# Loading q and k of six retention steps in natural order of heads, with a PSUM bank of its own for the state's products

## The chip, the cores and the metric

The kernel runs on one core of a Trainium2 chip. The metric is the device time of one execution in microseconds (us). Before the change three runs took 658.92, 657.10 and 658.42 us, median 658.42 us. One more execution was recorded by the hardware profiler.

The engines are named as in the profile: PE (TensorE; PEld is its weight load), DVE (VectorE), ACT (ScalarE), POOL (GpSimd) and SP (SyncE, which here only issues transfers).

## The reference

```
# retention, batch 4, heads 8, sequence 768, head size 64
state = zeros(B, H, D, D)
for t in range(S):
    state = gamma[h] * state + k[:, :, t] (outer) v[:, :, t]
    y[:, :, t] = q[:, :, t] @ state / sqrt(D)
# then a feed-forward block on x = y as (3072, 512)
h = x @ w_in                  # 512 x 2048
g = h / (1 + exp(-1.702 * h))
out = g @ w_out               # 2048 x 512
```

gamma is 1 - 2^-(5+h) of head h. The data are float32; the two weight matrices reach the kernel as 64-bit values, which it narrows to float32 on the chip.

## The kernel before

**Tiles.** The sequence is cut into 12 chunks of 64 positions; one step works on one chunk of two batches, all eight heads. There are 24 steps. Steps 0 to 11 are batches 0 and 1, steps 12 to 23 are batches 2 and 3. Four steps make a block of 512 tokens, and the feed-forward block follows on such blocks (up, gate, down), with products saved by Strassen-like sums.

**Two layouts.** Steps 0 to 5 (`j < NEW`, NEW = 6) hold q, k and v with the position on the partitions: partitions 0 to 63 are the first batch, 64 to 127 the second; the eight heads lie along the free dimension. From step 6 on, the partition halves are groups of four heads instead, and q and k are loaded already turned. `halves_anew` (L938) moves the state, the mask and the decays from the one layout to the other, once, after step 5.

**One step of the first layout**, in the names of the code:
- `load` (L131): q on SP's queue, k on POOL's queue (step 0: ACT's), v on SP's queue (L146). For q and k each batch half goes in two transfers, one per group of four heads, and they interleave the groups, so that head n of the tile is head s of group 0, then head s of group 1. v goes in natural order, one transfer a half.
- `turn` (L246): PE transposes pairs of neighbouring heads of the tile (L255); `turned` copies them from PSUM on ACT (L266). With the interleaved order a pair is heads s and s + 4.
- `decay` (L268): ACT scales k by the chunk's decay, one instruction a head (L277).
- `attend` (L286) puts the products on PE, 16 of 64x64x64 each: attention scores (L294), the state's update k'v (L302), the share of y that comes from the old state (L311) and the local share (L317). The array is used as four tiles, rows half by columns half. Scores and update go to the two banks of `pa`, both shares of y to the two banks of `py`. In all four groups the row half decides the bank, and every group uses all four tiles.
- `masked` (L321), `by_state` (L326), `output` (L338) and `updated` (L366) run on DVE, `aged` (L356) on ACT (steps 0 to 5).

**PSUM.** `pa` and `py` hold two banks each. The remaining four are `ps`: two tags, `x` and `y`, of two buffers in turn. Transposes use `y`; the feed-forward's up products `ph` use `x` and `y` (`unit`, L981).

**What sets the order.** PE's and most other instructions around the change are kept in program order (`pin`). For steps 0 to 7 that order is written out by hand, as a list of names (L997 to L1015): for example `step5-4` is the scores of step 5 with the rest of step 4, `step-3` the rest of step 3 alone, `turn`, `turned`, `decay`, `masked`, `state`, `x`, `aged`, `updated` are the functions above, `up0.th.p` and `gate0.th.p` are an up product and its gate, `w3a` a load of weights (L186), and `abs3`, `half3`, `rest3` the parts of its narrowing (ACT L212, DVE L216 to L227). The narrowed weights' raw bytes go through three buffers (`RAWS`, L175), so that a weight load waits for an earlier narrowing. The change leaves this list alone.

Of the kernel before, what the change touches and what calls it, by code (L numbers as in the profile page):

```python
# [9 lines left out]
F32 = mybir.dt.float32  # L10
U32 = mybir.dt.uint32
AF = mybir.ActivationFunctionType
ALU = mybir.AluOpType
P = 128
# [14 lines left out]
def kernel(  # L29
# [94 lines left out]
    def pin(i):  # L124
        return tc.keep_in_program_order(i) if ordered[0] else i


    NEW = 6
    QKV = {}

    def load(j, what="qkv"):  # L131

        b, c = j // NC * 2, j % NC
        rows = slice(c * D, (c + 1) * D)
        keep = tc.keep_in_program_order if j < 2 * CB else lambda i: i

        def plain(name, src, tag, bufs, engine=sp):
            t = two.tile([P, H, D], F32, name=name + "_in", tag=tag, bufs=bufs)  # L140
            QKV[name, j] = t
            for i in range(2):
                if j < NEW:
                    to, at = t[i * D:(i + 1) * D], src[b + i, :, rows, :].rearrange("h p d -> p h d")
                    for n in range(1 if name == "v" else 2):
                        keep(engine.dma_start(*((to, at) if name == "v" else (to[:, n:H:2], at[:, n * HP:(n + 1) * HP]))))  # L146
                else:
                    for r in range(2):
                        keep(engine.dma_start(t[r * D:(r + 1) * D, i * HP:(i + 1) * HP],
                                              src[b + i, r * HP:(r + 1) * HP, rows, :].rearrange("h p d -> p h d")))  # L150

        if j < NEW:
            if "q" in what:
                plain("q", q, "q_sq", 2)
            if "k" in what:
                plain("kn", k, "k_sq" if j in (0, 1, 4, 5) else "o", 2, pool if j else act)
        elif "q" in what:
            for name, src in (("q", q), ("k", k)):
# [70 lines left out]

    QT, KT, KD, AT, TURNED, PA, PU, PY, SHARE = [{} for _ in range(9)]
    HALF = [slice(i * D, (i + 1) * D) for i in range(2)]
    TWO = [(i, r) for i in range(2) for r in range(2)]

# [32 lines left out]
    def decay(j):  # L268

        if j % NC == NC - 1:  # L270
            return
        KD[j] = home(j, "kd")
        x = QKV["kn", j]
        if j < NEW:

            for h in range(H):
                pin(act.activation(KD[j][:, h], x[:, h % HP * 2 + h // HP], AF.Copy, scale=cold[:, H + h:H + h + 1]))  # L277
        else:
            pin(pool.tensor_mul(KD[j].rearrange("p (i s) d -> p i s d", i=2), x.rearrange("p (i s) d -> p i s d", i=2),
                                cold[:, None, H:H + HP, None].to_broadcast([P, 2, HP, D])))  # L280

    def by_half(t, j):

        return t.rearrange("p s (w t) -> p w s t" if j < NEW else "p (w s) t -> p w s t", w=2)

    def attend(j, f=None):  # L286

        pa = ps_a.tile([P, 2, 2, HP, D], F32, name="pa", tag="pa")
        if j is not None:
            PA[j] = pa  # L290
            kt, qt = by_half(KT.pop(j), j), by_half(QT[j], j)
            for s in range(HP):
                for u, w in TWO:
                    pe.matmul(pa[HALF[w], u, 0, s, :], kt[HALF[u], w, s, :], qt[HALF[u], w, s, :], start=True, stop=True)  # L294
        if f is not None:
            c = f % NC
            old, vn, a, qt = state[c % 2], QKV.pop(("v", f)), AT.pop(f), by_half(QT.pop(f), f)
            if c < NC - 1:
                kd = KD.pop(f)
                for s in range(HP):  # L300
                    for w, u in TWO:
                        pe.matmul(pa[HALF[u], w, 1, s, :], kd[HALF[w], HP * u + s, :], vn[HALF[w], HP * u + s, :],  # L302
                                  start=True, stop=True)


            py = ps_a.tile([P, 2, 2, 4, D], F32, name="py", tag="py")
            if c:
                for s2 in range(2):
                    for w in range(2):
                        for u, o in TWO:  # L310
                            pe.matmul(py[HALF[o], u, 1, 2 * w + s2, :], old[HALF[u], w, 2 * s2 + o, :],  # L311
                                      qt[HALF[u], w, 2 * s2 + o, :], start=True, stop=True)
            for s2 in range(2):
                for u in range(2):
                    for w, o in TWO:
                        s = 2 * s2 + o
                        pe.matmul(py[HALF[o], w, 0, 2 * u + s2 if f < NEW else 2 * s2 + u, :],  # L317
                                  vn[HALF[w], HP * u + s, :], a[HALF[w], u, s, :], start=True, stop=True)
            PU[f], PY[f] = pa[:, :, 1], py

    def masked(j):  # L321
        AT[j] = home(j, "at")
        pin(dve.tensor_mul(AT[j], PA.pop(j)[:, :, 0],
                           mask if j < NEW else mask[:, 0:1].to_broadcast([P, 2, HP, D])))

    def by_state(f):  # L326

        if f < NEW:
            SHARE[f] = tmp = two.tile([P, 2, 4, D], F32, name="tmp", bufs=1)
            pin(dve.tensor_mul(tmp.rearrange("p i a t -> p i (a t)").rearrange("p i (r t) -> p i r t", r=2),  # L330
                               PY[f][:, :, 1].rearrange("p r (i s) t -> p i r (s t)", i=2),
                               rowd.rearrange("p (r s) t -> p r (s t)", r=2)[:, None].to_broadcast([P, 2, 2, P])))
        else:
            SHARE[f] = tmp = two.tile([P, 4, 2, D], F32, name="tmp", bufs=1)
            pin(dve.tensor_mul(tmp.rearrange("p a i t -> p i a t"), PY[f][:, :, 1],
                               rowd[:, None].to_broadcast([P, 2, HP, D])))

    def output(f):  # L338
# [14 lines left out]
        else:  # L353
            pin(act.activation(x, y, AF.Copy))

    def aged(f):  # L356

        c = f % NC
        old, new = state[c % 2], state[(c + 1) % 2]
        if f < NEW:  # L360
            for s in range(HP):
                pin(act.activation(new[:, :, s], old[:, :, s], AF.Copy, scale=whole[:, s:s + 1]))
        else:
            pin(pool.tensor_mul(new.rearrange("p r s d -> p (r s) d"), old.rearrange("p r s d -> p (r s) d"),
                                whole_h[:, :, None].to_broadcast([P, H, D])))

    def updated(f):
        c = f % NC
        new, u = state[(c + 1) % 2], PU.pop(f)
        if c == 0:  # L370
            pin(dve.tensor_copy(new, u))
        elif c < NC - 1:
            pin(dve.tensor_add(new, new, u))
# [553 lines left out]
    def lay_whole():  # L927

        for r in range(2):
            pin(pool.dma_start(  # L930
                whole[HALF[r]], bass.AP(tensor=col_decay.tensor, offset=col_decay.offset + (D - 1) * W + H + HP * r,
                                        ap=[[0, D], [1, HP]])))

    def late_loads():
        load(2 * CB, "qkv")
# [2 lines left out]
    def halves_anew():  # L938

        pin(pool.dma_start(whole_h, bass.AP(tensor=col_decay.tensor, offset=col_decay.offset + (D - 1) * W + H,  # L940
                                            ap=[[0, P], [1, H]])))
        pool.tensor_copy(mask[HALF[1], 0], mask[HALF[1], 1])
        pool.tensor_copy(cold[HALF[1], H:H + HP], cold[HALF[1], H + HP:2 * H])
        old, new = state[NEW % NC % 2], state[(NEW + 1) % NC % 2]
        for u in range(2):
            pool.dma_start(new[HALF[1 - u], u], old[HALF[u], 1 - u])
        for u in range(2):
            pool.tensor_copy(old[HALF[u], 1 - u], new[HALF[u], 1 - u])

    works |= {  # L950

# [159 lines left out]
```

## Time and profile before

| | before |
|---|---|
| median of three runs | 658.42 us |
| the profiled execution's own time | 659.02 us |
| its span | 657.3 us |
| PE busy | 639.0 us (97%) |
| DVE busy | 437.9 us (67%) |
| ACT, POOL busy | 166.6 us, 182.0 us |
| DMA packets | 148149, 131600 of them under 512 B |

The span runs from the program's first instruction to its last; 1.7 us of the execution lie outside it. The page divides the span into 40 slices of 16.4 us and gives each engine's busy share in tenths, the clock that was granted to PE, and the mean busy share of the 16 DMA engines. An engine's idle time costs something only where the end of the program follows from it. PE's busy time is that of pipelined products, so a busy PE may still be slowed by a lower clock. The chain of work that ended last follows from each instruction back to what released it; it names a DMA where a landing was waited for, and a queue (SPq, ACTq) where an issue was.

### The profile page before, as it was taken

What the parts mean: (1) busy time and instruction counts of PE and PEld (TensorE: products, weight loads), DVE (VectorE), ACT (ScalarE), POOL (GpSimd) and SP (SyncE); (2) the same over time, 40 slices, a digit from 0 to 9 for tenths busy, and PEclk for the clock granted to TensorE, in tenths of its full rate; (3) what the DMA queues carried; (4) which work ended last, traced back from release to release, by engine and by line L of the source; (5) the groups of instructions that cost most, each with busy time, mean ns of one, the idle gap of its engine ahead of it and who ended that gap; (6) DMA issues with size and microseconds to landing.
All of it is one profiled execution on the core that took longest, in us unless ns stands there. A gap on an engine that the chain in (4) does not pass through costs nothing.

```text
span 657.3 us, 15175 instructions
## 1 busy us (share of the span) xinstructions
PE 639.0 (97%) x6390; PEld 577.0 (88%) x6390; DVE 437.9 (67%) x609; ACT 166.6 (25%) x320; POOL 182.0 (28%) x210
## 2 busy tenths in 40 slices
PE   6789999999999999999999999999999999999997
PEld 2678888888888888889999888999888999988997
DVE  3699989999936963348885246987245986144854
ACT  4574334551000000333100333110333110333210
POOL 6400311310478218000636200535300334300000
PEclk9899999999999999999999999999999999999999
DMA  9997549854233465541567821387831244501142
GB/s 168 189 256 207 152 102 233 220 127 62 49 92 146 119 155 150 192 135 42 155 161 205 246 40 49 114 196 180 257 59 49 77 140 153 205 24 49 52 158 97
DMA packets 148149, 89.77 MB, mean 137 GB/s; under 512 B 131600, under 2 KB 134416, under 8 KB 147056
## 3 DMA queue, kind: packets, MB, share of 16 engines
q1 hardware_dynamic: 135856, 44.66, 30.3%
q0 software_dynamic: 9456, 38.16, 18.5%
q10 hardware_dynamic: 2768, 5.96, 2.6%
q8 instruction: 50, 0.82, 0.5%
q14 instruction: 19, 0.16, 0.1%
HBM read 71.32 MB, written 14.94 MB: 131 GB/s over the span
## 4 chain that ended last, share of the span: by engine, by line
PE 89%; DMA 6%; DVE 2%; SPq 1%; issue 0%; ACT 0%; ACTq 0%; DVEq 0%
PE pq L717 27%; PE px L590 17%; PE pd L852 15%; PE pz L590 8%; PE ph L488 6%; PE ph L417 4%; PE py L590 4%; DMA W<-in_moe_w_in_dram 2%; PE pa L294 2%; PE py L317 1%; DMA G<-in_moe_w_in_dram 1%; PE py L311 1%; DMA W<-in_moe_w_out_dram 1%; PE pa L302 1%; PE pb L488 1%; DMA kn_in<-in_k_dram 1%
## 5 line engine op out<-in xcount | busy, mean ns | idle before, releaser
L692 POOL DMA_DIRECT2D LATE<-W2D x28 | 15.5, 555 | 245.6 <-PE pq L717 124.0
L717 PE MATMUL pq<-W,G 128*128 128x128 f32 x672 | 80.2, 276 | 0.0
L717 PEld LDWEIGHTS pq<-W,G 128*128 128x128 f32 x672 | 77.6, 192 | 0.6
L590 PE MATMUL px<-X,W1A 128*128 128x256 f32 x256 | 60.5, 379 | 0.0
L590 PE MATMUL px<-X,LATE 128*128 128x256 f32 x256 | 60.5, 379 | 0.0
L717 PE MATMUL pq<-LATE 128*128 128x128 f32 x448 | 59.8, 276 | 0.0
L417 PE MATMUL ph<-X,W1A 128*128 128x256 f32 x256 | 57.4, 382 | 1.2 <-DVE X L352 0.8
L417 PEld LDWEIGHTS ph<-X,W1A 128*128 128x128 f32 x256 | 48.0, 190 | 8.1 <-DVE X L352 0.9
L717 PEld LDWEIGHTS pq<-LATE 128*128 128x128 f32 x448 | 54.5, 192 | 0.4
L590 PEld LDWEIGHTS px<-X,LATE 128*128 128x128 f32 x256 | 48.6, 190 | 6.6
L590 PEld LDWEIGHTS px<-X,W1A 128*128 128x128 f32 x256 | 48.4, 190 | 6.5
L852 PE MATMUL pd<-W,G 128*128 128x256 f32 x224 | 49.6, 381 | 0.0
L852 PEld LDWEIGHTS pd<-W,G 128*128 128x128 f32 x224 | 42.2, 190 | 5.9
L398 ACT ACTIVATE G<-G 128x512 f32<-128x512 f32 x49 | 30.8, 629 | 45.3 <-DVE G L645 19.7
L635 DVE TENSOR_TENSOR G<-pz,vv 128x512 f32<-128x512 f32 x16 | 11.1, 692 | 46.7 <-ACT vv L605 46.6
L852 PE MATMUL pd<-W,LATE 128*128 128x256 f32 x160 | 35.2, 380 | 0.0
L852 PEld LDWEIGHTS pd<-W,LATE 128*128 128x128 f32 x160 | 30.2, 190 | 4.3 <-DVE LATE L574 0.2
L739 ACT ACTIVATE o<-pq 128x512 f32<-128x512 f32 (+1 forms) x14 | 7.6, 545 | 91.3 <-PE pq L717 91.3
L590 PE MATMUL pz<-X,W1A 128*128 128x256 f32 x128 | 30.3, 379 | 0.0
L590 PE MATMUL py<-X,W1A 128*128 128x256 f32 x128 | 30.2, 379 | 0.0
L590 PE MATMUL pz<-X,LATE 128*128 128x256 f32 x128 | 30.2, 379 | 0.0
L717 PE MATMUL pq<-W,LATE 128*128 128x128 f32 x224 | 29.7, 275 | 0.1
(210 smaller groups left out, 1169.6 us busy)
## 6 DMA issues: line engine op xcount, KB each, us to landing
LATE<-W2D POOLq DMA_DIRECT2D x28, 768.0 KB, 4.8
W<-in_moe_w_in_dram SPq DMA_DIRECT2D x12, 512.0 KB, 5.2
W<-in_moe_w_out_dram SPq DMA_DIRECT2D x10, 512.0 KB, 5.7
out_dram<-o POOLq DMA_DIRECT2D x20, 256.0 KB, 3.5
q_sq<-in_q_dram SPq DMA_DIRECT2D x144, 32.0 KB, 2.3
k_sq<-in_k_dram SPq DMA_DIRECT2D x144, 32.0 KB, 2.2
v_in<-in_v_dram SPq DMA_DIRECT2D x72, 64.0 KB, 2.7
LATE<-W1D ACTq DMA_DIRECT2D x3, 1536.0 KB, 7.4
```

The source lines that it names most:

```text
L294: pe.matmul(pa[HALF[w], u, 0, s, :], kt[HALF[u], w, s, :], qt[HALF[u], w, s, :], start=True, stop=True)
L302: pe.matmul(pa[HALF[u], w, 1, s, :], kd[HALF[w], HP * u + s, :], vn[HALF[w], HP * u + s, :], start=True, stop=True)
L311: pe.matmul(py[HALF[o], u, 1, 2 * w + s2, :], old[HALF[u], w, 2 * s2 + o, :], qt[HALF[u], w, 2 * s2 + o, :], start=True, stop=True)
L398: pin(act.activation(g, h[:, i], AF.Gelu_apprx_sigmoid))
L417: pe.matmul(h[:, ab], w, X[:, 2 * th + c // 2, c % 2, :], start=(ab == 0 and c == 0), stop=(c == 3), skip_group_check=True)
L488: pe.matmul(acc[:, u, :], w, x, start=(start and u == 0 and c == 0), stop=(stop and c == 1), skip_group_check=True)
L590: pe.matmul(acc[:, u, :], w1(2 * d + u, sw)[:, c, :], X[:, sx, c, :], start=(start and u == 0 and c == 0), stop=(stop and c == 1), skip_gr ...
L635: dve.tensor_add(a[3], z, v)
L692: engine.dma_start(c, W2D[i])
L717: pe.matmul(p0[:, j, :], a[:, d], w[:, d], start=(new and j == 0 and d == 0), stop=(d == NP // 2 - 1), skip_group_check=True)
L739: act.activation(to, y, AF.Copy)
L852: pe.matmul(p0[:, n, :], g1(m, p, sa)[:, n * P:(n + 1) * P], W2[:, sb, p, :], start=(new and p == 0 and n == 0), stop=(last and p == NP - ...
```

## The change

The loads of q and k of steps 0 to 5 take the heads as they lie: one transfer for each batch half instead of two, 24 transfers less (12 on SP's queue, 10 on POOL's, 2 on ACT's), each of 128 KB instead of 64 KB. A tile then pairs heads 2s and 2s+1. The partition half u of the state holds heads 2s + u instead of 4u + s, and what depends on it follows: the mask is read in another order, `whole` is loaded with a step of two, the update's products take head 2s + u.

With this pairing the old state's share of y must land on the partition half that its head's state lies on, so each of those 16 products goes from row half u to column half u. They get a bank of their own, `sr`, out of the pool `ps` (tag `x` in steps 1 to 3, `y` in steps 4 and 5), and DVE reads it there. The products' order becomes: update, the old state's share, the local share, as before. `held` gives the buffer that holds the state; from step 6 on the two buffers change places, because `halves_anew` now writes all four quarters to the other buffer (two by DMA, in runs of 256 B, two by POOL's copies, which no longer read what the DMAs write).

```
@@ load
-                    for n in range(1 if name == "v" else 2):
-                        keep(engine.dma_start(*((to, at) if name == "v" else (to[:, n:H:2], at[:, n * HP:(n + 1) * HP]))))
+                    keep(engine.dma_start(to, at))
@@ decay
-                pin(act.activation(KD[j][:, h], x[:, h % HP * 2 + h // HP], AF.Copy, scale=cold[:, H + h:H + h + 1]))
+                pin(act.activation(KD[j][:, h], x[:, h], AF.Copy, scale=cold[:, H + h:H + h + 1]))
@@ attend
-            old, vn, a, qt = state[c % 2], QKV.pop(("v", f)), AT.pop(f), by_half(QT.pop(f), f)
+            old, vn, a, qt = held(f), QKV.pop(("v", f)), AT.pop(f), by_half(QT.pop(f), f)
...
-                        pe.matmul(pa[HALF[u], w, 1, s, :], kd[HALF[w], HP * u + s, :], vn[HALF[w], HP * u + s, :],
+                        h = 2 * s + u if f < NEW else HP * u + s
+                        pe.matmul(pa[HALF[u], w, 1, s, :], kd[HALF[w], h, :], vn[HALF[w], h, :],
                                   start=True, stop=True)
             py = ps_a.tile([P, 2, 2, 4, D], F32, name="py", tag="py")
+            PU[f], PY[f] = pa[:, :, 1], py
+            if f < NEW:
+                if c:
+                    SR[f] = sr = ps.tile([P, 2, HP, D], F32, name="sr", tag="x" if f < CB else "y")
+                for s in range(HP if c else 0):
+                    for w in range(2):
+                        for u in range(2):
+                            pe.matmul(sr[HALF[u], w, s, :], old[HALF[u], w, s, :], qt[HALF[u], w, s, :],
+                                      start=True, stop=True)
+                for s in range(HP):
+                    for w, u in TWO:
+                        pe.matmul(py[HALF[u], w, 0, s, :], vn[HALF[w], 2 * s + u, :], a[HALF[w], u, s, :],
+                                  start=True, stop=True)
+                return
@@ masked
-                           mask if j < NEW else mask[:, 0:1].to_broadcast([P, 2, HP, D])))
+                           m3.rearrange("p (s u) t -> p u s t", u=2) if j < NEW else mask[:, 0:1].to_broadcast([P, 2, HP, D])))
@@ by_state
-            pin(dve.tensor_mul(tmp.rearrange("p i a t -> p i (a t)").rearrange("p i (r t) -> p i r t", r=2),
-                               PY[f][:, :, 1].rearrange("p r (i s) t -> p i r (s t)", i=2),
-                               rowd.rearrange("p (r s) t -> p r (s t)", r=2)[:, None].to_broadcast([P, 2, 2, P])))
+            pin(dve.tensor_mul(tmp, SR.pop(f), rowd[:, None].to_broadcast([P, 2, HP, D])))
@@ aged, updated
+    def held(f, n=0):
+
+        return state[(f + n + (f >= NEW)) % 2]
...
@@ lay_whole: offset "+ r" and step 2 in place of "+ HP * r" and step 1
@@ halves_anew
-        old, new = state[NEW % NC % 2], state[(NEW + 1) % NC % 2]
+        old, new = held(NEW - 1, 1), held(NEW).rearrange("p r (s u) d -> p u (r s) d", u=2)
         for u in range(2):
             pool.dma_start(new[HALF[1 - u], u], old[HALF[u], 1 - u])
         for u in range(2):
-            pool.tensor_copy(old[HALF[u], 1 - u], new[HALF[u], 1 - u])
+            pool.tensor_copy(new[HALF[u], u], old[HALF[u], u])
```

More of the change, by code (lines that the diff above doesn't have):

```diff
@@ L227, in rest @@
             pin(dve.tensor_add(self.w, b, a))
-    QT, KT, KD, AT, TURNED, PA, PU, PY, SHARE = [{} for _ in range(9)]
+    QT, KT, KD, AT, TURNED, PA, PU, PY, SR, SHARE = [{} for _ in range(10)]
     HALF = [slice(i * D, (i + 1) * D) for i in range(2)]
@@ L316, in attend @@
                         s = 2 * s2 + o
-                        pe.matmul(py[HALF[o], w, 0, 2 * u + s2 if f < NEW else 2 * s2 + u, :],
+                        pe.matmul(py[HALF[o], w, 0, 2 * s2 + u, :],
                                   vn[HALF[w], HP * u + s, :], a[HALF[w], u, s, :], start=True, stop=True)
-            PU[f], PY[f] = pa[:, :, 1], py
     def masked(j):
@@ L354, in output @@
             pin(act.activation(x, y, AF.Copy))
+    def held(f, n=0):
+        return state[(f + n + (f >= NEW)) % 2]
     def aged(f):
-        c = f % NC
-        old, new = state[c % 2], state[(c + 1) % 2]
+        old, new = held(f), held(f, 1)
         if f < NEW:
@@ L368, in updated @@
         c = f % NC
-        new, u = state[(c + 1) % 2], PU.pop(f)
+        new, u = held(f, 1), PU.pop(f)
         if c == 0:
@@ L930, in lay_whole @@
             pin(pool.dma_start(
-                whole[HALF[r]], bass.AP(tensor=col_decay.tensor, offset=col_decay.offset + (D - 1) * W + H + HP * r,
-                                        ap=[[0, D], [1, HP]])))
+                whole[HALF[r]], bass.AP(tensor=col_decay.tensor, offset=col_decay.offset + (D - 1) * W + H + r,
+                                        ap=[[0, D], [2, HP]])))
     def late_loads():
```

## The prediction

> **What bounds the kernel now.** I read the page's engine shares and slices first, to see where PE is idle; then the stretches that this suggests; then the chain in order of time, for what ends the waits there; then the transfers and the products that are edited.
>
> ```profile
> PE 639.0 (97%) x6390; PEld 577.0 (88%) x6390; DVE 437.9 (67%) x609; ACT 166.6 (25%) x320; POOL 182.0 (28%) x210
> ...
> PE   6789999999999999999999999999999999999997
> ...
> DVE  3699989999936963348885246987245986144854
> ```
>
> PE is busy everywhere but in the first three slices (49 us). The same in stretches (PE, PEld, DVE, ACT, POOL busy us; granted clock; DMA share; GB/s):
>
> ```profile
> 2.00:4.00 2.00, 0.10 (x1) 0.10 (x1) 0.00 (x0) 0.16 (x1) 1.92 (x6) 1.00 0.70 147
> 4.00:10.00 6.00, 3.47 (x8) 1.55 (x9) 0.00 (x0) 1.32 (x2) 4.71 (x8) 1.00 1.07 207
> 10.00:19.00 9.00, 8.98 (x112) 5.05 (x110) 5.32 (x8) 5.57 (x20) 5.46 (x9) 1.00 1.25 183
> 19.00:29.00 10.00, 6.22 (x172) 5.48 (x173) 6.63 (x11) 5.81 (x13) 5.39 (x9) 0.83 1.19 210
> 29.00:37.00 8.00, 5.69 (x134) 4.82 (x137) 7.28 (x9) 6.98 (x24) 0.00 (x0) 1.00 1.07 237
> ```
>
> From 4 to 37 us the transfers keep the 16 DMA engines over 100% busy (packets overlap); from 37 to 60 PE (21.73 of 23 us) and DVE (21.33) are both near full, and so to 94; after that PE alone carries the time. So an edit counts by how much earlier or later PE passes 94 us. The chain (start, us, what) names what paces the front:
>
> ```profile
> 10.12 8.73 DMA W<-in_moe_w_in_dram
> ...
> 18.87 9.45 DMA G<-in_moe_w_in_dram
> ...
> 31.91 5.24 DMA W<-in_moe_w_in_dram
> ```
>
> The reader is to see three landings in a row, w0a, w2a and w3a of the weights (ahead of w0a stands k of step 0, 6.29 us to its landing at 9.46). ACT's L212 and DVE's L216 to L227 narrow each, and from w2a on (half2 starts at 29.58) DVE hardly rests until 92. Their issues wait too: SP and ACT share eight semaphores in turn, so an issue waits for the landing of the transfer eight before it. w2a went out at 18.87 because w0a landed at 18.85.
>
> **The transfers.** Issue costs, ns, min/median/max:
>
> ```profile
> L146 SPq DMA_DIRECT2D q_in<-in_q_dram x24: 596/615/3915, 0.8 to 36.0; - x24
> L146 POOL DMA_DIRECT2D kn_in<-in_k_dram x20: 617/627/717, 3.8 to 25.5; - x20
> L146 SPq DMA_DIRECT2D v_in<-in_v_dram x12: 596/602/1213, 6.9 to 44.2; - x12
> ```
>
> v's 128 KB costs one issue of 0.6 us, like q's 64 KB. The change therefore takes 12 x 0.615 = 7.4 us off SP's queue, 10 x 0.627 = 6.3 us off POOL's and 2 x 0.69 (ACT's median) = 1.4 us off ACT's. But issue is not what these transfers spend their time on: q's take a median 6.2 us from issue to landing, v's 8.2, k's on POOL 7.2, so a queue of work stands before the DMA engines. Bytes and the 256 B runs stay. An issue that leaves a full queue earlier lands no earlier.
>
> The queue isn't full at the start. From 2 to 4 us only 147 GB/s moved, at a share of 0.70, while SP and ACT put out 64 KB per 0.65 us each. With 128 KB an issue, this stretch could move the 207 GB/s of the next: (207 - 147) x 2 us = 0.12 MB, or 0.6 us at 190 GB/s. w0b goes out at 2.3 instead of 3.80, behind two issues instead of four. And SP no longer stands between w0a and w2b: a dip near 20 us, where w2b has just been issued (17.74, landing 24.81), may fill for some 0.3 us. I take 0.9 us earlier for w0a, w2a and w3a alike. The ends: nothing (0), if DMA's work after 4 us is all that counts; and 3.9 us, if w0a lands as much earlier as it is issued (four issues of 0.6 us and a 1.9 us wait of SP's for k of step 0 go; it would leave near 6.2 instead of 10.12).
>
> POOL's queue: `causal`, which ends at 15.33, comes about 1 us earlier with w0b, then `whole` (2 x 0.55), k3 (2 x 0.63) and k of steps 4 and 5, which go out at 16.6 to 18.5 instead of 18.8 to 26. These 512 KB now compete with w2b and w2a. Of them 384 KB landed after w2a's 28.31; at 210 GB/s they are 1.8 us. I take nothing, since POOL's transfers are in flight throughout 18 to 33 us in either order and share with SP's by turns; at worst w2a is 1.8 us later, 0.9 net of the gain.
>
> ACT loses two issues before L952, hidden: ACT then waits for w0b until 10.19. k of step 0 lands near 6 instead of 9.46, and the turn of step 0, `rows` and the scores of step 0 move up by some 3 us; but step 1's scores (21.93) wait for DVE's `updated0` (21.10), queued behind half0a, which waits for w0a. So PE only waits longer there. Its granted clock is already at half from 21.6 to 25.0, after 2.95 us of idling (L294 takes 1.06 instead of 0.62 us for PE's advance); a longer idle time may stretch that by one such period, which the wait for w2a's narrowing covers (PE idles 0.81 us at 28, DVE 1.56 us at 29.6): 0, at worst 0.6.
>
> The trace puts the price on the engines, 256 B at a time. The Trainium skill, "DMA: Bandwidth & Descriptors", Rules for kernel authors, says to coalesce many small transfers, as below 64 KB one pays mostly for overhead. By that rule alone SP's 7.4 us would be the gain.
>
> **The products of the old state.** Here the change adds work. Step 5's, from the order of time (start, busy us):
>
> ```profile
> 70.37 0.65 PE L311 MATMUL py<-G,state 64*64 64x64 f32 x32
> ...
> 70.83 0.65 PE L317 MATMUL py<-G,v_in 64*64 64x64 f32 x32
> ...
> 71.55 0.69 DVE L330 TENSOR_TENSOR tmp<-py,rowd 128x512 f32<-128x512 f32 x1 [0.68 <-PE py L317]
> ```
>
> 16 products are 32 instructions and advance PE by 0.47 us (70.37 to 70.83), on four array tiles: eight each, 59 ns apart. `sr` uses two tiles, so 16 each: 0.94 us, 0.47 more, in steps 1 to 5. The ends: 0, if the 14.7 ns from one instruction to the next is an issue limit; and 32 x 59 = 1.89 us, 1.42 more, if the two row halves also can't write one bank together, which no group of this trace does. I take 0.47, the nearest reading.
>
> Where it lies: in step 1 PE then waits for X until 28.08 (0.81 us idle), in step 2 for `updated2` until 36.73 (1.17), in step 3 for rest3 until 44.89 (0.36 after 0.17): covered, exactly in step 3. Step 4's 0.47 at 54.5 is on PE's unbroken path to step 5. There DVE waits 0.68 us for L317, since `py` was one tile; now it needs `sr` alone, which ends at 70.31 + 0.47 + 0.94 = 71.72, plus 0.03 for the start: 71.75 against 71.55, +0.2. Behind that wait stand `updated5`, `output`, rest4, the weight issue at 76.58 and the q and k loads that SP issues after it; k lands at 92.0 and L258 lets PE go on at 94.11 after 0.89 idle. PE itself arrives 0.94 later, at 94.16. So +0.2 at 94 us. If DVE did not wait there, the cover of 0.89 would be gone all the same and the sum would be +0.05.
>
> The Trainium skill, "TensorEngine Tiling (Array Packing)", Gotcha 1, speaks against this: row tiles write different PSUM banks and can't access one bank at the same time. By it the 1.89 us would hold; by the row, 0.94. Here the two row tiles write different partitions of the bank, of which the page says nothing.
>
> **Banks.** `sr` takes turns in `x` and `y`. Its tightest waits: `up0.0.2` (37.36) then needs `gate0.0.0` done (35.02), `up0.1.2` (about 48.5) `state3` (45.44), step 5's `sr` (70.3) `state4` (60.93). Cost 0 with 2.3 us to spare; if PE's part came 2.3 us earlier than ACT's, the difference.
>
> **The rest.** L277, L323 and L330 keep counts and shapes (0.34 us a head, 0.69 and 0.69 us); L352, already strided, takes the same 0.68, so other strides cost 0 (0 to 0.1 each). In `halves_anew` POOL's copies lose a wait of 1.72 us for the DMAs, whose runs get shorter (2.15 us to landing, at worst 1 more); their reader, step 7's part at 94, is 15 us off. 0.
>
> Sum: -0.9 + 0.2 = -0.7 us, or 659.02 - 0.7 = 658.3 for the profiled execution (span 657.3 and 1.7 around it). That one is 0.6 above the median, so 657.7 against 658.42.
>
> **The rivals.** A: the issues were the limit, not the engines. For it: w2a's issue waits on w0a's landing. Against it: DMA shares of 1.07 to 1.25, landings 6 to 9 us after issue. w0a 3.9 us earlier, +0.2: 654.7.
> B: row halves serialise on `sr`'s bank, and the kernel gets slower. Step 3 loses 1.1 of its 1.42 us (0.53 covered, 0.25 left from step 2), and in step 5 `sr` ends at 70.78 + 1.42 (step 4's) + 1.42 = 73.62, where DVE starts now at 71.55: +2.1. Together +3.2 - 0.9: 660.7. It decides from 0.73 us more a group, some 1.2 us for the 32 instructions, where the total passes zero.
> C: POOL's earlier k loads delay w2a by 1.8, and with it DVE's unbroken work: +0.9 + 0.2: 659.5.
> D: the transfers are hidden entirely, only +0.2 stays: 658.6.
>
> **How the numbers follow.** Forecast 0.33, A in whole or in part 0.23, B 0.19, C 0.13, D 0.12. About 0.3% (2.0 us) is what a measurement of this kernel tells from no change. Faster by more: most of A, some of the forecast, 0.26. Slower by more: most of B, a third of C, 0.25. Same: 0.49. The range runs from most of A, 655.0, to B, 661.0; the forecast's own is 656.5 to 659.
>
> **What would show it.** Right: w0a and w2a issued 4 us earlier or more, but landing within 1.5 us of before; `sr`'s 32 instructions in 0.9 us; DVE's wait for PE at step 5 below 1 us; PE past 94 at 93 to 94. Wrong: a landing of w2a outside 26.8 to 29.8, a group of 1.4 us or more, or a new idle time of PE before an `up0` product that waits for a bank.

## The result, and the profile after

| | before | after |
|---|---|---|
| median | 657.76 us (6 runs, 654.84 to 658.92) | 662.91 us (6 runs, 661.23 to 664.35) |
| ratio | | 1.0082, interval 1.0056 to 1.0107 |
| the profiled execution | 659.02 us, span 657.3 | 662.38 us, span 660.7 |
| DMA packets | 148149 | 147765 |

The kernel is slower by 5 us, where 0.7 us less was forecast and 661.0 was the upper end of the range. The two medians for before (here six runs, the prediction had three) differ by 0.66 us; single runs of one kernel lie up to 3.9 us from their median (before: 2.9), and a trace shows one run.

The page's shares and slices after the change, the same rows as before:

```profile
PE 643.0 (97%) x6390; PEld 581.2 (88%) x6390; DVE 437.2 (66%) x609; ACT 166.6 (25%) x320; POOL 177.2 (27%) x200
...
PE   6799999999999999999999999999999999999997
...
DVE  3589889999936874357885246986245986144854
```

PE has the same number of instructions and is busy 4.0 us longer. The rows below name two things that fit, a lower clock and the state's products on two tiles; their shares were not measured. The stretches of the front (PE, PEld, DVE, ACT, POOL busy us; granted clock; DMA share; GB/s):

```profile
2.00:4.00 2.00, 0.10 (x1) 0.11 (x1) 0.00 (x0) 1.48 (x2) 1.92 (x6) 1.00 0.85 164
4.00:10.00 6.00, 3.73 (x10) 1.81 (x10) 0.39 (x1) 1.10 (x3) 2.52 (x4) 1.00 1.14 212
10.00:19.00 9.00, 8.27 (x110) 4.51 (x109) 6.23 (x11) 6.54 (x23) 5.72 (x9) 1.00 1.15 173
19.00:29.00 10.00, 5.85 (x145) 5.34 (x149) 4.63 (x8) 3.05 (x8) 2.03 (x3) 0.73 0.88 183
29.00:37.00 8.00, 8.00 (x95) 6.69 (x89) 6.99 (x9) 7.49 (x24) 0.00 (x0) 0.69 1.06 202
```

Up to 10 us the transfers run as foreseen: 164 and 212 GB/s, against 147 and 207. Then 173 against 183, and from 19 to 29 us the DMA share is 0.88 where it was 1.19, with 183 GB/s instead of 210. PE's clock was at half from 20.2 to 23.6 and from 27.1 to 33.9; before only from 21.6 to 25.0.

The chain in order of time (start, us, what):

```profile
1.60 7.59 DMA kn_in<-in_k_dram
...
16.41 12.85 DMA G<-in_moe_w_in_dram
...
32.95 7.20 DMA W<-in_moe_w_in_dram
```

The second is w2a, as before. It leaves 2.46 us earlier (16.41, was 18.87) and takes 12.85 us instead of 9.45, so that it lands 0.95 us later. w3a (the third) lands at 40.16, 3.0 us later. From there the delay is carried to the end almost unchanged: the scores of step 7 start at 96.84 instead of 94.11, the first `pq` product at 310.36 instead of 307.63 (2.73 both), the span ends 3.36 later.

**The hole.** Between w2a's issue and its landing something takes the DMA engines away. The stretches in single microseconds, after:

```profile
18.00:19.00 1.00, 0.27 (x20) 0.13 (x10) 0.93 (x3) 0.99 (x4) 1.00 (x3) 1.00 0.79 11
19.00:20.00 1.00, 0.00 (x0) 0.01 (x1) 0.88 (x2) 0.81 (x2) 1.00 (x2) 1.00 0.00 0
20.00:21.00 1.00, 0.98 (x33) 0.88 (x33) 0.00 (x0) 0.00 (x0) 0.34 (x1) 0.62 0.99 1
21.00:22.00 1.00, 1.00 (x7) 1.00 (x6) 0.93 (x2) 0.00 (x0) 0.47 (x1) 0.50 0.46 56
```

and the same of before:

```profile
18.00:19.00 1.00, 0.98 (x60) 0.84 (x52) 0.00 (x0) 0.13 (x1) 1.00 (x3) 1.00 1.30 183
19.00:20.00 1.00, 0.00 (x0) 0.00 (x0) 0.43 (x1) 1.00 (x3) 1.00 (x2) 1.00 1.32 181
20.00:21.00 1.00, 0.00 (x0) 0.00 (x0) 0.94 (x2) 0.99 (x4) 0.14 (x1) 1.00 0.95 187
21.00:22.00 1.00, 0.07 (x4) 0.10 (x7) 0.78 (x2) 0.74 (x2) 0.08 (x1) 0.78 1.05 287
```

The last number is what the reader is to see: 11, 0, 1 and 56 GB/s where it was 183, 181, 187 and 287. The 16 engines moved 0.07 MB in 4 us instead of 0.84 MB (the sums of these rows), while w2a, issued at 16.41, and k of steps 3 to 5, from 16.25 on, stood before them. What is under way in that time can be read from the single packets of the trace. `whole` is 2 KB in both kernels, two transfers on POOL's queue, 32 packets of 64 B:

| `whole`'s packets | number | median ns | longest | first start to last end, us |
|---|---|---|---|---|
| before | 32 | 13 | 24 | 18.0 to 20.2 |
| after | 32 | 1097 | 2506 | 17.3 to 22.7 |

Here the change turned 128 runs of 16 B (a partition's four decays, one beside the other) into 512 runs of 4 B (every second of eight decays). The issue takes 0.62 us each, near the 0.55 that was forecast. From 18.61 to 21.65 us no packet of another load starts; at 19 us only `whole`'s are under way, five of them, and from 20.5 on ten and more. So the hole is tied to these packets, but why the engines without one move nothing either is not shown. Of `whole` in the view by tile, before:

```profile
L930 POOL DMA_DIRECT2D whole<-in_col_decay_dram x2: 548/551/554, 15.3 to 15.8; - x2
...
  ACT state L362: 0.3, 1
```

and after:

```profile
L944 POOL DMA_DIRECT2D whole<-in_col_decay_dram x2: 615/625/635, 15.0 to 15.6; - x2
...
  ACT state L376: 3.4, 1
```

ACT's `aged` waits 3.4 us for it (0.3 before), and in the order of time PE stands still in the middle of step 1's products of the old state:

```profile
27.82 0.37 PE L314 MATMUL sr<-G,state 64*64 64x64 f32 x2 [3.12 <-issue]
```

**The products of the state**, step 5's (start, busy us):

```profile
73.59 1.03 PE L314 MATMUL sr<-G,state 64*64 64x64 f32 x29
...
74.77 0.69 DVE L343 TENSOR_TENSOR tmp<-sr,rowd 128x512 f32<-128x512 f32 x1 [0.68 <-PE sr L314]
```

The products of `py` follow at 74.43, so that the group advances PE by 0.84 us (0.47 before). DVE waits 0.68 us for it, as before, and starts 1.18 us behind the group's first product, as before (70.37 to 71.55).

The issues of the loads, ns, min/median/max:

```profile
L145 SPq DMA_DIRECT2D q_in<-in_q_dram x12: 595/732/5742, 0.8 to 37.1; - x12
...
L145 POOL DMA_DIRECT2D kn_in<-in_k_dram x10: 682/691/722, 3.8 to 19.7; - x10
```

One issue of q took 5.74 us (25.66 to 31.40), behind the hole.

### The profile page after: what moved, and what is told of

Read it like the earlier page. It is cut to its first block, busy times and chain, and to the rows that moved or that the text cites. A ratio compares the mean times of both kernels' runs of the same rounds, so it can differ in the third digit from the quotient of the medians.

```text
span 660.7 us, 15131 instructions
## 1 busy us (share of the span) xinstructions
PE 643.0 (97%) x6390; PEld 581.2 (88%) x6390; DVE 437.2 (66%) x609; ACT 166.6 (25%) x320; POOL 177.2 (27%) x200
## 2 busy tenths in 40 slices
DMA packets 147765, 89.76 MB, mean 136 GB/s; under 512 B 131216, under 2 KB 134032, under 8 KB 146672
## 4 chain that ended last, share of the span: by engine, by line
PE 92%; DMA 4%; DVE 1%; SPq 1%; ACT 0%; issue 0%; ACTq 0%
PE pq L731 27%; PE px L604 17%; PE pd L866 15%; PE pz L604 8%; PE ph L431 8%; PE ph L502 6%; PE py L604 4%; DMA G<-in_moe_w_in_dram 2%; PE pa L293 2%; PE py L331 1%; PE pa L302 1%; PE py L325 1%; DMA kn_in<-in_k_dram 1%; DMA W<-in_moe_w_in_dram 1%; PE pb L502 1%; SPq L185 1%
## 5 line engine op out<-in xcount | busy, mean ns | idle before, releaser
L431 PE MATMUL ph<-X,W1A 128*128 128x256 f32 x256 | 59.3, 391 | 1.3 <-DVE W1A L226 1.3
L431 PEld LDWEIGHTS ph<-X,W1A 128*128 128x128 f32 x256 | 49.4, 195 | 8.9 <-DVE W1A L226 1.6
```

The costliest lines, as they stand in the source:

```text
L431: pe.matmul(h[:, ab], w, X[:, 2 * th + c // 2, c % 2, :], start=(ab == 0 and c == 0), stop=(c == 3), skip_group_check=True)
```

## The experiments

In the tables, before stands for runs of the kernel before on the same chip: median 657.95 us (29 runs) for the first four kernels (`after` in their table is the row of the result above, against its own 657.76), 657.58 (13) for the kernel with 64 rows and the three of the last table, 657.98 (19) for the other two. A ratio is estimated from all single runs, so it is not exactly that of the two medians.

### Which part of the change costs the 5 us

Theory 1: the short runs of `whole`. The rival: the loads in another order of heads, which bring POOL's k loads forward (case C of the prediction), or the products on two tiles (case B). The first kernel is after with `whole` filled from one load of 32 B runs that the kernel makes anyway for later (`whole_h`, moved up), and two ACT copies:

```diff
     def lay_whole():
+        pin(pool.dma_start(whole_h, bass.AP(tensor=col_decay.tensor, offset=col_decay.offset + (D - 1) * W + H,
+                                            ap=[[0, P], [1, H]])))
         for r in range(2):
-            pin(pool.dma_start(
-                whole[HALF[r]], bass.AP(tensor=col_decay.tensor, offset=col_decay.offset + (D - 1) * W + H + r,
-                                        ap=[[0, D], [2, HP]])))
+            pin(act.activation(whole[HALF[r]], whole_h[HALF[r], r:H:2], AF.Copy))
...
     def halves_anew():
-        pin(pool.dma_start(whole_h, bass.AP(tensor=col_decay.tensor, offset=col_decay.offset + (D - 1) * W + H,
-                                            ap=[[0, P], [1, H]])))
```

> The changed kernel with `whole` filled in another way: one load of 32 B rows (whole_h's, moved up from halves_anew) and two copies on ACT take the place of two loads in runs of 4 B. Theory 1 (the 4 B runs of `whole` stop the DMA engines from 18 to 21 us and hold up ACT's aged1, w2a and PE's instructions): `whole` lands within 7 us of its issue, no stretch of 1 us between 18 and 22 moves under 100 GB/s, PE has no 3.1 us idle time inside step 1's products, and the time is within 1.5 us of the kernel before. Theory 2 (the old state's products on two array tiles carry the loss): PE idles less at 25 us, but the time stays 3 to 5 us over before. Theory 3 (fewer and larger transfers fill the queues deeper and land later): the time stays 3 us or more over before and w2a lands after 28 us.

The second is before with nothing but the two transfers of `whole` from after:

```diff
-                whole[HALF[r]], bass.AP(tensor=col_decay.tensor, offset=col_decay.offset + (D - 1) * W + H + HP * r,
-                                        ap=[[0, D], [1, HP]])))
+                whole[HALF[r]], bass.AP(tensor=col_decay.tensor, offset=col_decay.offset + (D - 1) * W + H + r,
+                                        ap=[[0, D], [2, HP]])))
```

> The kernel before with one edit: `whole` is loaded with the changed kernel's two transfers (every second head, runs of 4 B), so its decays are those of other heads. Theory 1: a stretch near 18 to 22 us with next to no DMA traffic, aged1 and the weights later, +3 to +5 us. Theories 2 and 3: no change, within 0.7 us.

The third is before with the 24 transfers less and nothing else:

```diff
-                    for n in range(1 if name == "v" else 2):
-                        keep(engine.dma_start(*((to, at) if name == "v" else (to[:, n:H:2], at[:, n * HP:(n + 1) * HP]))))
+                    keep(engine.dma_start(to, at))
```

> The kernel before with the 24 transfers less alone (q and k in natural order); the transposes then pair neighbouring heads while v and the state keep the old pairing, so heads are mixed up and the numbers are not the reference's; all instructions and shapes on PE, DVE and ACT are those of before. Theory 1 with the prediction's sum for the transfers: 0.5 to 2 us faster than before. Theory 3: 2 us or more slower. Theory 2: no change, within 0.7 us.

The fourth is the first (32 B runs) with the state's products put back on four tiles and into `py`:

```diff
-                for s in range(HP if c else 0):
-                    for w in range(2):
-                        for u in range(2):
-                            pe.matmul(sr[HALF[u], w, s, :], old[HALF[u], w, s, :], qt[HALF[u], w, s, :],
-                                      start=True, stop=True)
+                    for s2 in range(2):
+                        for w in range(2):
+                            for u, o in TWO:
+                                pe.matmul(py[HALF[o], u, 1, 2 * w + s2, :], old[HALF[u], w, 2 * s2 + o, :],
+                                          qt[HALF[u], w, 2 * s2 + o, :], start=True, stop=True)
...
-            pin(dve.tensor_mul(tmp, SR.pop(f), rowd[:, None].to_broadcast([P, 2, HP, D])))
+            pin(dve.tensor_mul(tmp, PY[f][:, :, 1], rowd[:, None].to_broadcast([P, 2, HP, D])))
```

> e1_row with the old state's products written as before (four array tiles, row half decides the bank of py, no bank sr); half of the heads' shares land on the wrong partitions, so the numbers are not the reference's. It prices the two-tile products: their group takes 0.47 us instead of 0.85. Theory 1: 0.2 to 0.9 us less than e1_row. Theory 2: 1.5 to 4 us less than e1_row.

| | median us (runs) | ratio to before | interval |
|---|---|---|---|
| after | 662.91 (6) | 1.0082 | 1.0056 to 1.0107 |
| after, `whole` by 32 B runs | 658.73 (12) | 1.0015 | 0.9999 to 1.0031 |
| before, `whole` by 4 B runs | 661.21 (6) | 1.0055 | 1.0034 to 1.0076 |
| before, 24 transfers less | 658.89 (12) | 1.0010 | 0.9993 to 1.0028 |
| after, 32 B runs, four tiles | 657.91 (12) | 1.0011 | 0.9994 to 1.0028 |

Taking the two transfers out of after takes 4.4 us away (0.0067 x 658; 4.2 by the medians); putting them into before adds 3.6 us. No other part has a price that its interval tells from nothing; the gain of 0.5 to 2 us that was expected of the 24 transfers less did not come. One sign of theory 1 failed too: PE still stands for 2.42 us inside step 1's products when `whole` comes by 32 B runs. The single microseconds of after with 32 B runs, where the hole was:

```profile
19.00:20.00 1.00, 0.63 (x33) 0.59 (x33) 0.22 (x1) 0.80 (x3) 0.00 (x1) 1.00 1.02 297
20.00:21.00 1.00, 1.00 (x13) 0.85 (x8) 0.88 (x2) 0.97 (x4) 0.00 (x0) 1.00 1.06 389
```

and of before with the 4 B runs:

```profile
18.00:19.00 1.00, 0.00 (x0) 0.00 (x0) 0.93 (x3) 0.99 (x4) 1.00 (x3) 0.50 0.00 0
19.00:20.00 1.00, 0.00 (x0) 0.00 (x0) 0.91 (x2) 0.88 (x2) 0.48 (x1) 0.50 0.59 0
20.00:21.00 1.00, 0.94 (x32) 0.97 (x32) 0.00 (x0) 0.00 (x0) 0.00 (x0) 0.50 0.56 0
```

297 and 389 GB/s in the one; less than 1 GB/s for 3 us in the other. The hole follows the two transfers.

### Is it the size of the runs, or what they read?

A run of 4 B is short, but there is a second thing about it: all 64 partitions of a transfer read the same row, the last of `col_decay` (source step 0), so that 512 runs read the same 32 B, where 128 did before. Theory 1 is now the size, theory 2 the reads of one place. Before, with 4 B runs from another row for each partition:

```diff
-                whole[HALF[r]], bass.AP(tensor=col_decay.tensor, offset=col_decay.offset + (D - 1) * W + H + HP * r,
-                                        ap=[[0, D], [1, HP]])))
+                whole[HALF[r]], bass.AP(tensor=col_decay.tensor, offset=col_decay.offset + H + r,
+                                        ap=[[W, D], [2, HP]])))
```

> The kernel before, with whole's two transfers in 4 B runs, but each partition reads its own row of col_decay instead of all of them the last row (whole holds other values than the decays, so the output is not the reference's). Theory 1, the size of the runs: as where all partitions read one row, the 16 DMA engines move under 20 GB/s for some 3 us between 18 and 22 us, whole's packets take 0.3 to 2.4 us, and the time is 3.6 us above before (1.0035 to 1.0075). Theory 2, 512 reads of the same eight addresses: packets of well under 0.3 us, no stop of the engines, and a ratio of 1.000 to 1.002.

The ratio is 1.0010 (0.9990 to 1.0029; 657.76 us, 10 runs). The 32 packets take 12 to 25 ns, median 22, and there is no hole:

```profile
18.00:19.00 1.00, 0.00 (x0) 0.00 (x0) 0.90 (x3) 1.00 (x3) 1.00 (x3) 0.50 1.17 174
19.00:20.00 1.00, 0.00 (x0) 0.00 (x0) 1.00 (x2) 0.96 (x3) 0.29 (x1) 0.50 1.08 237
20.00:21.00 1.00, 0.59 (x21) 0.62 (x25) 0.26 (x1) 0.63 (x3) 0.56 (x1) 0.50 1.07 291
```

So theory 1 falls: 512 runs of 4 B in packets of 64 B cost nothing that these runs can tell (at most 0.29%). The trace bears on another rival, the clock: PE's clock was at half for 10.2 us here, as long as in after, and this execution took 656.70 us. So that much time at half clock need not cost anything. Two more kernels come at it from both sides. The first keeps 4 B runs that all partitions share, but takes a partition's four runs from four rows that lie 1 KB apart, so that each place is read 128 times:

```diff
-                whole[HALF[r]], bass.AP(tensor=col_decay.tensor, offset=col_decay.offset + (D - 1) * W + H + HP * r,
-                                        ap=[[0, D], [1, HP]])))
+                whole[HALF[r]], bass.AP(tensor=col_decay.tensor, offset=col_decay.offset + H + r,
+                                        ap=[[0, D], [16 * W, HP]])))
```

> The kernel before, with whole's 512 runs of 4 B on POOL's queue as in the kernel with these runs alone, but a partition's four runs come from rows 0, 16, 32 and 48 of col_decay (1 KB apart) instead of one row: each of the places is read by all partitions, 128 reads of a place instead of 512 of one (whole holds other values than the decays). Theory 1, reads of one place are served one after the other and the count per place decides: packets under 0.1 us, or a stop of at most 1 us, and a ratio of 1.000 to 1.003. Theory 2, any rows that all partitions share are slow together, the total of 512 shared reads decides: a stop of about 3 us and 1.0035 to 1.0075.

The second leaves `whole` as it was before and reads the one row 512 times more, in runs of 16 B, into a tile that nothing uses:

```diff
+            pin(pool.dma_start(
+                again[HALF[r]], bass.AP(tensor=col_decay.tensor, offset=col_decay.offset + (D - 1) * W + H + HP * r,
+                                        ap=[[0, D], [0, HP], [1, HP]])))
...
```

> The kernel before with whole untouched, and beside it two more transfers on POOL's queue that nothing reads: 512 runs of 16 B, all of the same 32 B of col_decay. Theory 1, the number of reads of one place decides, not the 4 B: the 16 DMA engines stop for some 3 us between 17 and 22 us, with packets of 1 us and more, and the ratio is 1.0035 to 1.0075. Theory 2, it takes runs of 4 B together with one place: packets under 0.2 us, no stop, 1.000 to 1.002 (two more issues of POOL's, 1.1 us).

| POOL's small transfers, on the kernel before | reads of one place | packets, median (longest) ns | ratio, interval |
|---|---|---|---|
| 16 B, one row (before) | 128 | 13 (24) | 1 |
| 4 B, one row | 512 | 1194 (2434) | 1.0055, 1.0034 to 1.0076 |
| 4 B, 64 rows | 8 | 22 (25) | 1.0010, 0.9990 to 1.0029 |
| 4 B, four rows | 128 | 21 (28) | 1.0010, 0.9990 to 1.0030 |
| 16 B, one row, beside `whole` | 512 more | 1668 (2922) | 1.0029, 1.0013 to 1.0046 |

("One place" counts the runs that begin within the same 32 B; nothing here tells how large a place is. The packets of the last row are those of the added transfers, 256 B with 16 runs each.) The runs of 16 B stop the engines too, though less completely and in two parts:

```profile
17.00:18.00 1.00, 0.00 (x0) 0.00 (x0) 0.93 (x2) 0.96 (x4) 1.00 (x3) 1.00 0.80 25
18.00:19.00 1.00, 0.00 (x0) 0.00 (x0) 0.94 (x2) 0.55 (x1) 1.00 (x2) 1.00 0.45 91
...
21.00:22.00 1.00, 1.00 (x6) 0.71 (x4) 0.97 (x2) 0.82 (x3) 0.61 (x1) 0.50 0.60 75
22.00:23.00 1.00, 1.00 (x53) 0.96 (x56) 0.72 (x2) 1.00 (x4) 0.00 (x0) 0.75 0.39 115
```

Their time stayed below what theory 1 of that run expected (1.0035 and more), though the intervals overlap. Nothing waits for the added tile, but ACT waits 2.6 us for `whole`, whose second transfer ran among the added packets. On POOL's queue, then, the number of reads of one place decides, not their size: 128 cost nothing that can be told, 512 stop the engines. Numbers in between were not tried, and the 512 reads were always of the last row.

The packets give a price for one read. In this last kernel, `whole`'s own second transfer ran in the middle of the others: nine of its packets, with four runs each, took exactly 306 ns, 76 ns a run. In the kernel with twice the 4 B runs (below) sixteen packets, with 16 runs each, took exactly 1209 ns, 76 ns a run again. All of `whole`'s packets together took 34.0 us in after and 34.4 in before with the 4 B runs, 66 to 67 ns a run. Shared among 16 engines that is an estimate of 2.1 us, of the order of the 3 us hole. But a run has no fixed price: a packet of after that had only three to five of its kind beside it (18.10 to 20.08 us) took 1.98 us, 124 ns a run. That the reads of one place are served one after the other is one reading of this; no run shows it, nor where it would happen.

### Does the queue matter, the place in the order, the number?

After, with `whole`'s two transfers on ACT's queue:

```diff
-            pin(pool.dma_start(
+            pin(act.dma_start(
```

> The kernel after, with whole's two transfers of 4 B runs issued on ACT's queue at the same place, not on POOL's. Theory 1, the size of the runs, whatever queue they come from: the stop of about 3 us stays and the ratio is 1.006 to 1.010. Theory 2, POOL's queue prepares its transfers in another way and the small runs are slow only there: the stop goes, the packets take under 0.1 us, and the ratio is that of the kernel with 32 B runs, 1.0015 (1.000 to 1.003).

After, with the two transfers at the very start of POOL's queue:

```diff
+        for r in range(2):
+            pin(pool.dma_start(
+                whole[HALF[r]], bass.AP(tensor=col_decay.tensor, offset=col_decay.offset + (D - 1) * W + H + r,
+                                        ap=[[0, D], [2, HP]])))
...
     def lay_whole():
-        for r in range(2):
...
+        pass
```

> The kernel after, with whole's two transfers moved to the start of POOL's queue, ahead of everything that POOL does. Theory 1, work of the engines that is taken from the transfers of the front: the stop moves to the first 8 us, lasts as long, and delays q, k and w0a instead, since all of the front up to 37 us is bound by the engines; the time stays 3 to 5 us above before (1.005 to 1.009). Theory 2, it is the place near 20 us that hurts (SP's issue behind it, the instruction fetch that lands in it, the turn of step 1): at the start, where the engines still have room (147 GB/s from 2 to 4 us), it costs half or less: 1.001 to 1.004.

After, with the two transfers issued a second time, into a tile that nothing reads:

```diff
+        for r in range(2):
+            pin(pool.dma_start(
+                again[HALF[r]], bass.AP(tensor=col_decay.tensor, offset=col_decay.offset + (D - 1) * W + H + r,
+                                        ap=[[0, D], [2, HP]])))
...
```

> The kernel after, with the same two transfers of 4 B runs issued once more into a tile that nothing reads. Theory 1, the runs' work on the engines: a second stop of about 3 us behind the first, w3a's narrowing 3 us later again, and a ratio of 1.012 to 1.016, that is 3 to 5 us above after. Theory 2, the first pair costs by what it delays (the wait of ACT, an instruction fetch of PE) and not by the engines' time: the second pair costs under 1.5 us, and the ratio is 1.008 to 1.010.

| | median us (runs) | ratio to before | interval |
|---|---|---|---|
| on ACT's queue | 663.75 (4) | 1.0093 | 1.0075 to 1.0110 |
| at the start | 665.05 (4) | 1.0114 | 1.0097 to 1.0131 |
| twice | 664.24 (4) | 1.0106 | 1.0083 to 1.0129 |

**ACT's queue.** Neither theory fits. The time is theory 1's, but the hole isn't there:

```profile
19.00:20.00 1.00, 0.00 (x0) 0.00 (x0) 0.93 (x3) 1.00 (x3) 0.36 (x1) 0.78 1.08 192
20.00:21.00 1.00, 0.00 (x0) 0.00 (x0) 1.00 (x2) 0.96 (x3) 0.00 (x0) 0.50 1.13 195
21.00:22.00 1.00, 0.83 (x32) 0.86 (x32) 0.02 (x1) 0.01 (x1) 0.00 (x0) 0.50 0.90 170
```

The trace shows the runs in another form, 512 single packets of 4 B with a median of 9 ns (longest 98), spread from 24.7 to 29.1 us. So 512 reads of one place do not stop the engines in this form. (From 38 to 40 us nothing moves there either, but then nothing is issued: SP issues nothing from 33.8 to 39.75.) What seems to cost here is that `whole` lands late:

```profile
L944 ACTq DMA_DIRECT2D whole<-in_col_decay_dram x2: 603/620/638, 18.1 to 18.8; - x2
...
  ACT state L376: 9.2, 1
...
DMA to landing us min/median/max: 11.3/11.3/11.4
```

ACT's first `aged` waits 9.2 us for it instead of 3.4, and the front stands behind that in the trace; no run took this wait away. On POOL's queue a packet has 16 reads; here each read is a packet by itself, with other transfers' packets between. Whether the spread over 4.4 us comes from taking turns or from the one place was not tried. The Trainium skill, "DMA: Bandwidth & Descriptors", Rules for kernel authors, says that a strided last dimension lowers to one descriptor per element and should be made contiguous. The 512 packets on ACT's queue agree. The kernel with 64 rows, which has as many runs on POOL's queue at no cost that can be told, shows that their number alone isn't the price there; on ACT's queue it was not tried.

**At the start.** The hole moves and seems to hurt more (7.5 us against 5 to 5.4, with intervals that overlap). The stretches there:

```profile
8.00:9.00 1.00, 1.00 (x7) 0.75 (x5) 0.00 (x0) 0.04 (x1) 0.00 (x0) 1.00 0.64 64
9.00:10.00 1.00, 1.00 (x3) 0.50 (x2) 0.35 (x1) 1.00 (x3) 0.00 (x0) 1.00 0.87 44
10.00:11.00 1.00, 1.00 (x2) 0.00 (x0) 0.93 (x3) 1.00 (x5) 0.00 (x0) 1.00 0.62 34
```

By 16 us, 2.28 MB had moved instead of 2.88 in after. So there was no room at the start: the transfers were issued at 3.2 but ran from 7.2 on, where the engines were already full. Theory 1 is right that it is work taken from a bound front; the price is above what either theory gave.

**Twice.** More stops are there (4 and 10 GB/s from 17 to 19 us, 68 and 25 from 20 to 22, 58 and 100 from 25 to 27), and by 36 us 6.00 MB had moved instead of 6.42; but the time rises by some 1.6 us (1.0106 against 1.0082, with intervals that overlap), between the two theories' figures. In the trace w3a's narrowing starts at 41.49 instead of 40.24 and step 7's scores at 98.09 instead of 96.84, both 1.25 later. The price does not grow in proportion to the stops.

No version tried is faster than before. After with 32 B runs, which computes the whole reference, is equal to it within the interval.

## Why the prediction was wrong

**The step that failed** is POOL's queue, in "`causal`, which ends at 15.33, comes about 1 us earlier with w0b, then `whole` (2 x 0.55)", together with "The rest", where other strides were costed at nothing from an operand of DVE (L352); the stride of `whole` lies on the DRAM side of a transfer. `whole` was priced by the time that POOL needs to issue it, and that nearly held (0.62 us each). Its transfer, 2 KB of 90 MB, got no line, no bounds and no cover. Put at nothing, it measures 4.4 us in after and 3.6 alone: the other loads stand still for 3 us, and w2a and w3a land later. The prediction bounds its other unseen terms from both sides ("The ends"); it did not do so for the one small load whose access on the DRAM side changed. The nearest row was `whole`'s landing of before, 6.3 us, which contains none of this; so the trace could not have given the number, but it could have given the reason for a wide upper end: the front is bound by the DMA engines, and this was the only transfer of the front whose number of runs rose (128 to 512).

**The transfers** (-0.9 us). The mechanism was half right. w0a left at 5.60 (forecast near 6.2) and landed at 16.89, 1.96 earlier, more than the 0.9 taken and just outside the 1.5 that was to confirm it; k of step 0 landed at 9.19, not near 6. With the 24 transfers less alone, w2a's narrowing started at 23.95 and w3a's at 35.52 (28.40 and 37.24 before). But the 12 runs give 1.0010, 0.9993 to 1.0028: a gain of more than 0.5 us is excluded, so the 0.9 is not there. Why landings that come earlier gain nothing stays open. One trace is no evidence for such shifts: before with 4 B runs from 64 rows, whose other loads are those of before, started the same two at 26.16 and 35.54. Rule and row were weighed here: coalescing small transfers (the Trainium skill, "DMA: Bandwidth & Descriptors", Rules for kernel authors) brought nothing that the 12 runs show, as the trace's waits before the engines had suggested.

**The products** (+0.47 a group, +0.2 at 94 us). The size was a little high: 0.84 us a group against 0.94 forecast. DVE's wait at step 5 stayed at 0.68 us (forecast below 1), so that the 0.2 did not come at that place. Two row tiles write one bank at the full rate of two tiles, and 1.89 us, the end by Gotcha 1 of the Trainium skill's "TensorEngine Tiling (Array Packing)", is out by this measurement: these row tiles write different partitions of the bank. What the term costs in all is not settled: 1.0015 with two tiles, 1.0011 with four, with intervals some eight times as wide as the difference.

**Banks, `halves_anew`.** No PE wait before an `up0` product names a bank. Nothing contradicts the 0.

**The clock.** A longer half-clock period was allowed for, at most 0.6 us and covered. In the front it became 10.2 us in all instead of 3.4, and the first up product (L431) then took 5.65 us instead of 3.72. But before with 4 B runs from 64 rows has 10.2 us at half clock too, without a hole and without a price that can be told. And before with the 4 B runs on one row loses its 3.6 us though its first up product runs at full clock, in 3.72 us. So the clock does not explain the loss, and a longer half-clock period does not need the hole.

**The rivals.** A (issues were the limit): out, by the kernel with 24 transfers less. B had the right sign and nearly the size (660.7), for a wrong reason: `sr`'s groups take 0.84 us, far from the 1.2 from which it decides. C (POOL's earlier k loads delay w2a) looks right in after, where w2a lands late; but after with 32 B runs has the same k loads and starts w2a's narrowing at 25.88, earlier than before's 28.40, and so does the kernel with 24 transfers less (23.95). Its price of 1.1 us lies within the interval of after with 32 B runs, so the times alone do not exclude it. D (the transfers are hidden) is what is left when `whole` is taken out: it forecast 0.2 us above before, and after with 32 B runs is 0.8 above (interval -0.1 to +2.0).

**The signs.** Of those named for wrong, a landing of w2a outside 26.8 to 29.8 did not show (29.26), and apart from step 1's, in the middle of which PE stood still, no group took 1.4 us. The one that told was "PE past 94 at 93 to 94": 96.84. The first two were chosen for the rivals; none looked at what the DMA engines moved, which shows the cause in one row.

## What to carry to other kernels

A constant that is spread over partitions by a source step of 0 is read from one place by every partition and every run. Count these reads when the layout changes, whatever the bytes: on POOL's queue 128 cost nothing that could be told here, and 512 all but stopped the DMA traffic for 3 us. Loading the row in one contiguous run a partition and picking from it on the chip avoided this (1.0015). Price a small transfer by what its packets take, not by its issue.

## What the runs showed of the hardware

- Reads of one place in DRAM, on POOL's queue: with 128 a packet of four runs took 13 ns, with 512 a packet of sixteen took 1.1 to 1.2 us (median) and up to 2.5 (in runs of 16 B beside `whole`: 1.7 and 2.9); the same 4 B runs from 64 rows, 22 ns. With twice the transfers, thirteen of the first sixteen packets stay below 25 ns and all later ones take 0.6 us or more.
- The same source pattern becomes 32 packets of 64 B on POOL's queue and 512 packets of 4 B on ACT's.
- PE's stop of 3.12 us inside step 1's products, which the view puts down to its issue, is not the hole itself: in after with 32 B runs there is one of 2.42 us at the same instruction. In both, a 16 KB packet of the instruction queue (50 in the span) starts about 2.7 us before PE goes on (25.12 and 27.82; 22.17 and 24.94). The Trainium skill, "Runtime: NRT & Kernel Launch", Instruction fetch mechanics, says that a sequencer fetches its instructions in blocks of 16 KiB over a DMA queue of its own and that the cost is mostly hidden; the packets agree. That PE waits for its instructions there is a reading of the two traces and was not tried.
